# Attention and two gated layers on one core: new tables for the order, the engines and the buffer slots

## The chip, the cores and the metric

The kernel runs on one core of a Trainium2 chip. The metric is the device time of one execution in microseconds (us): the median of the runs is 578.70 us (three runs: 578.62, 578.70 and 579.78 us).

## The reference, cut to what matters

```python
def _attn_ref(q, k, v):                       # B, H, S, D = 2, 8, 768, 64
    block, window = 32, 16
    k_sum = k.reshape(B, H, nb, block, D).max(axis=3)
    v_sum = v.reshape(B, H, nb, block, D).mean(axis=3)
    scores_l = scale * q @ k^T   where |i - j| < window, else -1e9
    scores_s = scale * q @ k_sum^T + log(block)
    a = softmax(concat(scores_l, scores_s))
    return a @ concat(v, v_sum)

def _moe_ref(x, w_in, w_out):                 # 1536 tokens, 512 -> 2048 -> 512
    h = x @ w_in
    return (h * clip(h + 3, 0, 6) / 6) @ w_out

def _moe2_ref(x, w_in, w_out):
    h = x @ w_in
    return (h * cos(h)) @ w_out

reference = _moe2_ref(_moe_ref(tokens(_attn_ref(q, k, v))))
```

## The kernel before, in words

**Attention.** The host hands in the 768 positions of a head pair in 12 windows of 96 (64 and 16 on either side). `k_prep` (L516) makes for one pair of heads the block maxima of the keys: two DVE reductions into `ks` (L524); where the keys come as one row (`kp`), three copies lay the windows into `kw` (L534), and one copy spreads the 24 maxima behind each window (L537). `v_sums` and `fill` do the like for the values. `att` (L543) is one unit: the scores (L555) go into two PSUM banks `s`; `soft` (L598) adds the mask and takes a row minimum on DVE (L606, four a unit and pair), exponentiates on ACT (L614), adds a guard and inverts the sums on DVE (L623 and L624, the pair `invert`), and multiplies `e` by them, "the normalisation" (L629, POOL or DVE). TensorE transposes `e` into bank `t` (L569), ACT or DVE copies that to `pt` (L572), and L580 multiplies by the values into the single bank `o`; a copy to `xh` (L593) and a subtraction into `xl` (L595) split the result into two parts that TensorE can multiply at full rate.

**The two layers.** Every matmul of the layers is three (high by high, high by low, low by high; L745 to L747, L821, L973). Weights arrive packed, are unpacked by ACT (L675) and DVE (L679, L683), and split by `parts` (L689 copy, L690 subtraction). After a first product, `post` (L754) computes the gate on ACT and DVE and splits it (L798 copy, L800 subtraction). `g2` and `evac` accumulate the second product and add it to the running sums (L862); the last of these go to the output.

**What sets the order.** Nothing is scheduled on the chip or by the framework. The program makes 2,579 steps, each with the engines that may run it and a cost on each. `Plan.run` (L337) then takes the table `ORDER` entry by entry: entry `x` is step `x // 5`, issued on engine `x % 5` (0 TensorE, 1 ACT, 2 DVE, 3 POOL, 4 a DMA). Each engine runs what it was given in that order and waits there for its inputs. `SLOTS` says which of a class's buffers each step's buffer is. The costs in the `op(...)` calls were read by the search that wrote the tables; `run` looks only whether the engine is among those allowed:

```python
        for x in ORDER:
            o, e = self.ops[x // 5], ENGINES[x % 5]
            assert e in o.engs and not o.wait
            ...
            o.fn(e)
```

Loads go out on SyncE's queue, the identity and the first two queries on ACT's (L450, L462). TensorE starts on the layers' first products while attention still runs: the 65th TensorE entry of the table before starts at 57.55 us.

Of the kernel before, what the change touches and what calls it, by code (L numbers as in the profile page):

```python
# [29 lines left out]
HT = 2  # L30
# [34 lines left out]
def consts():  # L65
# [161 lines left out]
)  # L227
SLOTS = dict(
    kp="1001",
    ks="10011101",  # L230
    kw="20132013",
    z="201021021001200102101202",
# [128 lines left out]
def body(ctx: ExitStack, tc: tile.TileContext, q, k, kg, v, vf, w_in1, w_out1, w_in2, w_out2, ident_d, mask_d, avg_d, out):  # L361
# [181 lines left out]
    def att(b, h, ps, zs, prio):  # L543
# [46 lines left out]
        def got():  # L590
            return res.t[:, 0:n * HT * P].rearrange("p (x c) -> p x c", x=n)
# [482 lines left out]
```

## Time and profile before

| | |
|---|---|
| median of three runs | 578.70 us |
| the profiled execution's own time | 578.94 us |
| its span | 577.2 us |
| TensorE busy | 557.3 us (97%) |
| DVE busy | 462.5 us (80%) |
| ACT busy | 324.6 us (56%) |
| POOL busy | 263.6 us (46%) |

All rows are of this one execution; 1.7 us of its time lie outside the span. Busy time is the union of an engine's instructions. Instructions of one engine overlap a little at their ends: on DVE the next one of a pair is often shown to start some 80 ns before the one ahead of it has ended. A group's mean is its instructions' own duration, waits not counted. The granted clock of TensorE (PEclk) is a share of 2.4 GHz, so 0.5 is 1.2 GHz.

### The profile page before, as it was taken

What the parts mean: (1) busy time and instruction counts of PE and PEld (TensorE: products, weight loads), DVE (VectorE), ACT (ScalarE), POOL (GpSimd) and SP (SyncE); (2) the same over time, 40 slices, a digit from 0 to 9 for tenths busy, and PEclk for the clock granted to TensorE, in tenths of its full rate; (3) what the DMA queues carried; (4) which work ended last, traced back from release to release, by engine and by line L of the source; (5) the groups of instructions that cost most, each with busy time, mean ns of one, the idle gap of its engine ahead of it and who ended that gap; (6) DMA issues with size and microseconds to landing.
All of it is one profiled execution on the core that took longest, in us unless ns stands there. A gap on an engine that the chain in (4) does not pass through costs nothing.

```text
span 577.2 us, 9078 instructions
## 1 busy us (share of the span) xinstructions
PE 557.3 (97%) x3290; PEld 461.1 (80%) x3290; DVE 462.5 (80%) x912; ACT 324.6 (56%) x681; POOL 263.6 (46%) x250
## 2 busy tenths in 40 slices
PE   3878999999999999999999999999999999999997
PEld 2567988888888888888888878888888888888885
DVE  4999988898689548763999889994999779986762
ACT  4888887275534313443457667765656576554440
POOL 2657634463565106523357585533533355722410
PEclk9989999999999999999999999999999999999999
DMA  8879920111413203230230033230213102200023
GB/s 279 310 262 318 331 70 9 38 36 67 126 64 109 74 0 110 75 109 1 74 109 1 1 110 110 74 109 1 73 55 125 41 0 76 108 1 0 19 91 111
DMA packets 17901, 53.06 MB, mean 92 GB/s; under 512 B 2240, under 2 KB 5696, under 8 KB 17856
## 3 DMA queue, kind: packets, MB, share of 16 engines
q1 hardware_dynamic: 17424, 52.15, 26.4%
q8 instruction: 26, 0.43, 0.3%
q10 hardware_dynamic: 432, 0.33, 0.2%
q14 instruction: 19, 0.16, 0.1%
HBM read 49.32 MB, written 3.15 MB: 91 GB/s over the span
## 4 chain that ended last, share of the span: by engine, by line
PE 92%; DVE 4%; ACT 1%; DMA 1%; issue 0%; POOL 0%; SPq 0%; DVEq 0%
PE acc L821 25%; PE s L821 21%; PE t L973 10%; PE h L973 10%; PE h L745 4%; PE h L746 4%; PE h L747 4%; PE o L973 3%; PE t L569 2%; PE s L555 2%; PE o L580 1%; PE o L747 1%; PE t L747 1%; PE t L745 1%; PE o L745 1%; PE o L746 1%
## 5 line engine op out<-in xcount | busy, mean ns | idle before, releaser
L821 PE MATMUL acc<-g,wo 128*128 128x512 f32 (+1 forms) x384 | 90.5, 365 | 0.0
L415 POOL TENSOR_SCALAR g<-r 128x512 fp32r<-128x512 f32 (+1 forms) x48 | 35.2, 735 | 116.7 <-DVE r L796 62.3
L420 POOL TENSOR_TENSOR g<-r,g 128x512 fp32r<-128x512 f32 (+1 forms) x48 | 67.1, 1401 | 30.4 <-ACT g L413 28.6
L821 PE MATMUL s<-wo,g 128*128 128x512 f32 x288 | 76.0, 389 | 0.0
L821 PE MATMUL acc<-wo,g 128*128 128x512 f32 x288 | 75.7, 389 | 0.0
L821 PEld LDWEIGHTS acc<-g,wo 128*128 128x128 f32 x384 | 66.5, 188 | 11.4 <-issue 0.2
L821 PEld LDWEIGHTS acc<-wo,g 128*128 128x128 f32 x288 | 54.0, 188 | 11.5 <-DVE pc L862 0.4
L821 PEld LDWEIGHTS s<-wo,g 128*128 128x128 f32 x288 | 54.1, 188 | 11.2
L821 PE MATMUL s<-g,wo 128*128 128x512 f32 x240 | 62.7, 389 | 0.0
L675 ACT ACTIVATE cu<-raw 128x512 f32<-128x512 f32 x64 | 42.1, 667 | 24.0 <-DVE cf L683 14.0
L821 PEld LDWEIGHTS s<-g,wo 128*128 128x128 f32 x240 | 45.0, 188 | 9.4
L420 DVE TENSOR_TENSOR g<-r,g 128x512 fp32r<-128x512 f32 (+1 forms) x52 | 45.9, 887 | 6.9 <-POOL g L415 4.0
L683 DVE SCALAR_TENSOR_TENSOR cf<-cu,cf 128x512 uint32<-128x512 uint32 x64 | 50.0, 792 | 0.9 <-ACT cu L675 0.4
L420 POOL TENSOR_TENSOR wi<-cf,wi 128x512 fp32r<-128x512 f32 x28 | 41.2, 1477 | 16.9 <-ACT wi L413 14.9
L777 ACT ACTIVATE r<-r 128x512 f32<-128x512 f32 x48 | 30.1, 629 | 30.5 <-DVE r L784 30.2
L413 ACT ACTIVATE g<-r 128x512 fp32r<-128x512 f32 (+1 forms) x52 | 32.5, 625 | 21.9 <-DVE r L784 12.7
L973 PE MATMUL t<-sx,wi 128*128 128x512 f32 x168 | 44.4, 389 | 0.0
L745 PE MATMUL h<-xh,wi 128*128 128x512 f32 (+1 forms) x112 | 42.0, 375 | 0.3 <-DVE r L784 0.3
L614 ACT ACTIVATE e<-e,sm 128x120 f32<-128x120 f32 x96 | 36.8, 386 | 9.7 <-DVE sm L606 7.7
L973 PE MATMUL h<-xh,wi 128*128 128x512 f32 x112 | 41.1, 389 | 0.0
L746 PE MATMUL h<-xl,wi 128*128 128x512 f32 (+1 forms) x112 | 40.4, 360 | 0.0
L784 DVE SCALAR_TENSOR_TENSOR r<-n,r 128x512 f32<-128x512 int32 x48 | 39.5, 827 | 0.8
(149 smaller groups left out, 1245.5 us busy)
## 6 DMA issues: line engine op xcount, KB each, us to landing
raw<-in_w_in_dram SPq DMA_DIRECT2D x32, 512.0 KB, 4.1
raw<-in_w_out_dram SPq DMA_DIRECT2D x32, 512.0 KB, 3.6
vw<-in_v_dram SPq DMA_DIRECT2D x8, 768.0 KB, 6.7
kw<-in_kw_dram SPq DMA_DIRECT2D x4, 720.0 KB, 6.6
z<-in_q_dram SPq DMA_DIRECT2D x22, 128.0 KB, 4.3
out_dram<-part SPq DMA_DIRECT2D x8, 256.0 KB, 2.1
kp<-in_k_dram SPq DMA_DIRECT2D x4, 400.0 KB, 4.1
y<-in_vt_dram SPq DMA_DIRECT2D x4, 384.0 KB, 4.4
```

Source lines behind the costliest of these rows:

```text
L413: nc.scalar.activation(out=out, in_=in_, func=ACTF.Copy, scale=scale)
L415: eng[e].tensor_scalar(out=out, in0=in_, scalar1=scale, scalar2=0.0, op0=ALU.mult, op1=ALU.add)
L420: eng[e].tensor_tensor(out=out, in0=in0, in1=in1.bitcast(F32), op=ALU.subtract)
L614: lambda e, x=x: nc.scalar.activation(out=e_.t[:, x, :], in_=e_.t[:, x, :], func=ACTF.Exp, scale=-1.0, bias=sm.t[:, x:x + 1], accum_out=sm ...
L675: lambda e: nc.scalar.activation(out=u.t, in_=raw.t.bitcast(F32)[:, :, 1], func=ACTF.Prelu, scale=2.0 ** -112, alpha=2.0 ** 32),
L683: lambda e: nc.vector.scalar_tensor_tensor(out=f().bitcast(U32), in0=u.t.bitcast(U32), scalar=3, in1=f().bitcast(U32), op0=ALU.logical_shi ...
L745: nc.tensor.matmul(out=o, lhsT=wh, rhs=hi, start=(kk == 0), stop=False)
L746: nc.tensor.matmul(out=o, lhsT=wh, rhs=lo, start=False, stop=False)
L747: nc.tensor.matmul(out=o, lhsT=wl, rhs=hi, start=False, stop=(kk == KT - 1))
L784: op({"DVE": t(0.056, 0.542)}, lambda e: nc.vector.scalar_tensor_tensor(out=out(), in0=a(), scalar=s, in1=b(), op0=o0, op1=o1), pr, r=rd, ...
L821: nc.tensor.matmul(out=o, lhsT=l, rhs=r, start=(c == 0 and z == 0), stop=(c == GS - 1 and z == 2))
L973: nc.tensor.matmul(out=bank.t, lhsT=stat(u), rhs=get(v), start=(first and q == z == 0), stop=(q == 1 and z == 2), skip_group_check=True)
```

## The change

All 2,579 entries of `ORDER` and the strings of `SLOTS` are replaced, and seven costs that the search read are set anew. The steps themselves, their arithmetic and their shapes stay.

```diff
 ORDER = (
-    24, 174, 14, 59, 4, 64, 27, 36, 209, 32, 9, 324, 177, 186, 191, 182, 196, 42, 47, 18, 409, 202, 52, 214, 90, 644,
...
+    24, 59, 4, 174, 209, 64, 36, 47, 43, 27, 9, 32, 14, 409, 53, 18, 90, 182, 196, 188, 177, 193, 127, 324, 107, 202,
...
 SLOTS = dict(
-    kp="1001",
-    ks="10011101",
+    kp="0101",
+    ks="11010010",
...
-        op({"PE": 0.79}, mm, prio, mode=3, r=["avg", (vws[b, p], 0)], w=[bank], take=[bank, x, y])
+        op({"PE": 0.82}, mm, prio, mode=3, r=["avg", (vws[b, p], 0)], w=[bank], take=[bank, x, y])
...
-        op({"PE": 0.17 + 0.4 * n}, score, prio, mode=1,
+        op({"PE": 0.2 + 0.39 * n}, score, prio, mode=1,
...
-            op({"PE": 0.39}, trans, prio + 0.5 * AS * HT * x, r=["ident", *((e_, y) for y in range(N4))], w=[tp], take=[tp, pt])
+            op({"PE": 0.405}, trans, prio + 0.5 * AS * HT * x, r=["ident", *((e_, y) for y in range(N4))], w=[tp], take=[tp, pt])
...
-        op({"ACT": 0.1 + 0.207 * n, "DVE": 0.075 + 0.266 * n}, lambda e: copy(e, hi, got()), prio, r=[res],
+        op({"ACT": 0.26 + 0.12 * n, "DVE": 0.075 + 0.266 * n}, lambda e: copy(e, hi, got()), prio, r=[res],
...
-        op({"DVE": 0.16}, invert, prio, w=sums)
+        op({"DVE": 0.42}, invert, prio, w=sums)
         op(
-            {"POOL": 0.98, "DVE": 0.57},
+            {"POOL": 0.99, "DVE": 0.63},
...
-        op({"ACT": t(0.125, 0.45), "POOL": t(0.15, 0.47)}, lambda e: copy(e, hi(), r()), pr, r=[rb], w=[(gb, 0)],
+        op({"ACT": t(0.125, 0.45), "POOL": t(0.53, 0.1)}, lambda e: copy(e, hi(), r()), pr, r=[rb], w=[(gb, 0)],
```

Decoded by the rule above, the two tables say this.

**Entries by engine, whole table:** DVE 790, then 792; ACT 583, then 565; POOL 241, then 257; TensorE 841 and DMA 124 in both.

**Entries ahead of TensorE's 66th, where the two differ** (before, then after):

| steps | DVE | POOL | ACT |
|---|---|---|---|
| normalisation (L629) | 4, 1 | 8, 11 | |
| copy of `t` to `pt` (L572) | 3, 0 | | 9, 12 |
| weights' low part (L690) | 3, 1 | 4, 6 | |
| copy of `o` to `xh` (L593) | 1, 4 | | 8, 5 |
| windows into `kw` (L534) | 2, 3 | 4, 6 | 6, 3 |
| maxima into `kw` (L537) | 4, 3 | 2, 3 | |
| copy to `y` (L503) | 2, 3 | | 2, 1 |
| weights' high part (L689) | | 6, 4 | 2, 4 |
| gate's high and low part (L798, L800) | | 7, 5 | 1, 2 |
| mask and minimum (L606), exp (L614), gate (L777), unpack (L675) | 53, 52 | | 65, 61 |

TensorE's own first 65 entries are the same steps but for one, in nearly the same order.

**The first entries.** Before: the loads of the first two pairs' keys go out first, then identity, query, mask, values; DVE has the maxima of the first pair (two), of the second pair (two), two windows of the first pair (L534), the spread maxima (L537) of the second pair and then of the first; ACT has one window of the first pair and three of the second; POOL has the two further masks (L452). TensorE's first entry, the first pair's scores, needs the spread maxima and all windows of the first pair. After: the loads are the first pair's keys, its query, the mask, and only then the second pair's keys; DVE has one window of the first pair, its two maxima, and then the second pair's two maxima; POOL has one window of the first pair, its spread maxima, the masks, and then two windows of the second pair; ACT has one window of either pair.

**The normalisation and the fill near 31 us.** In both tables one pair's `invert` (step 151) and normalisation (step 152) are on DVE, and the fill of `vw` (step 141, L513) is on POOL just behind the latter. Before, step 152 comes straight after step 151; after, one unpacking (L679) stands between them.

**The end.** In both tables the last two entries are a whole addition of 512 columns into an output tile (L862) and its store, behind the last entry of TensorE's.

## Rows read from the trace of the kernel before

**Rows 1.** Stretches: us, busy us (x instructions) by engine, PEclk, DMA share, GB/s.

```profile
0.00:14.43 14.43, 5.34 (x72) 3.86 (x76) 7.00 (x33) 7.01 (x23) 3.90 (x15) 1.00 0.81 279
14.43:28.86 14.43, 12.09 (x234) 8.27 (x226) 13.03 (x62) 11.97 (x41) 9.77 (x10) 1.00 0.89 310
28.86:43.29 14.43, 11.32 (x165) 9.24 (x166) 13.62 (x53) 12.06 (x48) 8.07 (x8) 0.88 0.76 262
43.29:57.72 14.43, 12.97 (x181) 11.34 (x180) 14.29 (x54) 12.22 (x40) 11.11 (x14) 1.00 0.92 318
57.72:72.15 14.43, 14.43 (x190) 13.78 (x191) 14.15 (x53) 12.02 (x41) 8.81 (x11) 1.00 0.91 331
...
sum 577.20, PE 557.27 PEld 461.12 DVE 462.46 ACT 324.56 POOL 263.63; mean PE 13.93 PEld 11.53 DVE 11.56 ACT 8.11 POOL 6.59
```

**Rows 2.** What TensorE waited for, whole span: total us, times, longest.

```profile
PE s L555 <- DVE kw L417: 7.8, 1, 7.8
PE o L580 <- DVE xl L420: 2.0, 3, 1.0
PE t L569 <- ACT xh L413: 1.8, 1, 1.8
PE s L555 <- DVE sm L606: 1.8, 3, 1.0
```

**Rows 3.** Timeline of the start: start us, us, engine, line, operation.

```profile
4.36 1.01 DVE L524 TENSOR_REDUCE ks<-kp 128x12 f32<-128x384 f32 x2 [3.45 <-DMA kp<-in_k_dram]
...
5.65 1.01 DVE L524 TENSOR_REDUCE ks<-kp 128x12 f32<-128x384 f32 x2 [0.28 <-DMA kp<-in_k_dram]
...
6.58 0.69 DVE L417 COPY kw<-kp 128x384 f32<-128x384 f32 x2
...
7.19 0.51 DVE L417 COPY kw<-ks 128x288 f32<-128x288 f32 x2
...
7.81 1.08 PE L555 MATMUL s<-kw,z 64*64 64x120 f32 x16 [7.81 <-DVE kw L417]
```

**Rows 4.** Groups by line and shape up to 57.55 us: busy us, mean ns.

```profile
L629 POOL TENSOR_TENSOR e<-e,sm 128x480 f32<-128x480 f32 x8 | 8.5, 1060 | 11.7 <-DVE sm L624 6.2 <-DVE sm L606 4.7 <-ACT vs L413 0.7
...
L683 DVE SCALAR_TENSOR_TENSOR cf<-cu,cf 128x512 uint32<-128x512 uint32 x8 | 5.6, 698 | 0.0
...
L420 POOL TENSOR_TENSOR wi<-cf,wi 128x512 fp32r<-128x512 f32 x2 | 2.9, 1436 | 0.1
...
L415 POOL TENSOR_SCALAR kw<-kp 128x384 f32<-128x384 f32 x4 | 2.4, 610 | 0.0
...
L417 DVE COPY pt<-t 120x512 f32<-120x512 f32 x3 | 2.1, 684 | 0.1
...
L420 DVE TENSOR_TENSOR wi<-cf,wi 128x512 fp32r<-128x512 f32 x2 | 1.3, 659 | 0.0
L415 POOL TENSOR_SCALAR kw<-ks 128x288 f32<-128x288 f32 x2 | 1.1, 556 | 0.4 <-PE o L580 0.2
...
L417 DVE CAST xh<-o 128x256 fp32r<-128x256 f32 x1 | 0.4, 425 | 0.0
```

**Rows 5.** Line L629 up to 58 us: min/median/max ns, first and last start.

```profile
L629 DVE TENSOR_TENSOR e<-e,sm x4: 647/826/1799, 14.1 to 51.4; 128x480 f32<-128x480 f32 x4
```

**Rows 6.** Timeline about 31 to 35 us.

```profile
31.52 1.47 POOL L415 TENSOR_SCALAR vw<-vs 24x1536 f32<-24x1536 f32 x1
31.69 1.80 DVE L629 TENSOR_TENSOR e<-e,sm 128x480 f32<-128x480 f32 x1
...
33.64 1.08 PE L569 MATMUL t<-ident,e 128*120 128x128 f32 x4 [1.79 <-ACT xh L413]
```

**Rows 7.** Whole span by shape: a copy that more entries put on POOL.

```profile
L413 ACT ACTIVATE wi<-cf 128x512 fp32r<-128x512 f32 x43 | 26.8, 627 | 18.7 <-DVE cf L712 8.2 <-DVE cf L683 7.5 <-PE h L746 2.0
...
L415 POOL TENSOR_SCALAR wi<-cf 128x512 fp32r<-128x512 f32 x17 | 13.5, 794 | 23.6 <-DVE cf L683 15.1 <-DVE cf L712 8.4
```

**Rows 8.** The last DVE instruction of the span.

```profile
573.32 0.69 DVE L862 TENSOR_TENSOR pc<-pc,s 128x512 f32<-128x512 f32 x1 [0.67 <-PE s L821]
```

More of the change, by code (lines that the diff above doesn't have):

```diff
@@ L86 @@
 ORDER = (
[140 rows of a table removed]
[140 rows of a table added]
 )
 SLOTS = dict(
-    kp="1001",
-    ks="10011101",
-    kw="20132013",
-    z="201021021001200102101202",
-    vw="12030123",
-    h="1011100001010101101001100110100111011010100110101001101001100110",
+    kp="0101",
+    ks="11010010",
+    kw="10231023",
+    z="020122012001120102121002",
+    vw="31201320",
+    h="0101100001010101101010011000100110011010100110101001101001100110",
     vs="01011000",
     y="00000000",
-    s="011001011010100101100101101010011001101101010110100110101001101010011001100110011010010110",
@@ L238 @@
-    e="202012102101202102102102",
-    sm="323201201201302003030231",
+    s="101001011010010101010110011001101001101010010110011010100101101001100110010110011001101010",
+    e="102102102101021012012012",
+    sm="322302301323121031032102",
     t="00000000000000000000000000000000000000000000000",
-    pt="010101001010010101011001",
+    pt="101011010101100101101001",
     o="000000000000000000000000000000000000000",
-    raw="1021021210210212101201020121202102201201012012102112002120102021",
@@ L244 @@
-    cu="0110101010101011101101011010101101101101010101010110110001010100",
-    cf="0101010001210210120211020120101212012201102011020201220102120210",
-    wi="341025670413173250644172635027450634427053167451603271425630",
-    wo="21304231042310432104312403124031",
-    n=(
-        "1001011100111001201212101210101211101022101112001120120202212120121021012110210102210102210100120210"
-        "10120122102012"
-    ),
-    r="0010010111002002010122102020100122102101101202010120210210210120021020210121020101201201012020212021",
@@ L253 @@
-    g="1302102330126175042381657862031548672164573028641035728461386057823146807845136278504125687320172456",
-    acc="01011010101101101010010110010101011010011011010101010011",
-    pc="2404314130",
-    sx="520134",
+    raw="2012101210021200210210122121101220201210021012012001202120102021",
+    cu="1001001010111010011101101000010011101001100111001010101001010100",
+    cf="1010101110201201201200120121021001210012102011020201221001201021",
+    wi="043125437160302675146401237565170423216374050632751434026715",
@@ new lines @@
+    wo="24031204321404312043104231042310",
+    n=(
+        "0001000011102211212200200122111222110121021011202212110122021202010210100122012201212112102200012110"
+        "12121020120202"
+    ),
+    r="1010011101102211100202210220020111110202110102100210021002101021021002010212020112010121120121021012",
+    g="1230013202134712465807132156327845160841257301864260783156323510786453260412356817041283751024768345",
+    acc="10011010001110100011100101110111101010101010101010011010",
+    pc="3412041423",
@@ L257 @@
+    sx="423051",
 )
```

278 rows, old and new, of the table ORDER are left out of this document.

## The prediction, made before the changed kernel was run

> **What bounds the kernel now.** I read the stretches first. In the first four of 14.43 us TensorE is busy 5.34, 12.09, 11.32 and 12.97 us; in the fifth, and in every later one but the last, it is busy throughout [rows 1]. So of 57.72 us it works 41.72 and idles 16.0; of the remaining 519.5 us it idles 3.9, and the last DVE instruction starts at 573.32 us [rows 8], so that is the tail. The matmuls are the same in both kernels, so the change can win or lose in three places only: in the 16.0 us ahead of 57.72 us, in the 3.9 us behind 573.3 us, and by breaking the cover between them.
>
> The list of waits says who causes the 16.0 us: 7.8 is the time to the first score, the rest is in pieces of 1.8 us and less, released mostly by DVE [rows 2]. DVE is the loaded engine there: 7.00 + 13.03 + 13.62 + 14.29 = 47.9 us busy of the 53.4 that follow its first input at 4.36 us [rows 1, 3], or 90%, where POOL has 32.9 of the whole 57.7. One row wants a second look: the transposes at 33.64 us waited 1.79 us, by the list for an ACT copy, but the normalisation that they read ran on DVE from 31.69 for 1.80 us, beside a POOL fill from 31.52 for 1.47 us [rows 6]; alone, the same normalisation takes 0.65 us [rows 5]. The stretch from 28.86 us is also the one with a mean granted clock of 0.88 [rows 1]; with levels of 1 and 0.5 that is 0.24 × 14.43 = 3.5 us at 1.2 GHz, worth 1.7 us of full-speed work.
>
> **The change, part by part.** The seven costs are read by the search alone; at run time they are worth nothing. What runs otherwise is the tables.
>
> *The start.* Before, the first scores at 7.81 us stood behind eight DVE instructions: both pairs' maxima (4.36 to 5.37 and 5.65 to 6.66), two window copies to 7.27 and two spreads of the maxima to 7.70 [rows 3]. After, DVE does one window (half of 0.69) and the first pair's maxima (1.01), and the spread is POOL's, 0.56 [rows 3, 4]: 4.36 + 0.35 + 1.01 + 0.56 = 6.28, and with the 0.1 us between the last copy and the scores of before, 6.4 us. That is 1.4 us earlier. The nearest bounds: DVE's and POOL's first windows read the same tile together, and if one shuts the other out for POOL's 0.61 us [rows 4], the gain is 0.8; an earlier landing of the first keys, now ahead of the second pair's, would add, but no row prices it and I take 0. Behind the spread POOL has the masks, which DVE needs after the scores, 1.08 us long, so they are covered. The second pair's keys are issued two places later; they were used from 5.65 us, and DVE has work until 5.7, so a landing at up to 6.2 costs only the second scores, which in any case wait until DVE has emptied the score banks of the first. The next loads of keys wait for the first pair's buffer, free earlier by as much. I take 1.4.
>
> *The relief of DVE up to the 66th entry of TensorE (57.55 us).* By the table of entries DVE loses three copies to `pt` (3 × 0.684), three normalisations (3 × 0.647, the undisturbed one), two low parts (2 × 0.659) and one spread (0.26, half of 0.51): 5.6 us [rows 3, 4, 5]. It takes on three copies to `xh` (3 × 0.425), one window (0.35) and one copy to `y`, which has no row of its own and is smaller than that to `xh` (0.3): 1.9 us. Net 3.7; with four instructions fewer, the 0.08 us by which neighbours overlap is not saved four times: 3.4. As DVE is 90% loaded and releases most of TensorE's waits, I count the whole of it, with 0 and 3.4 as its bounds: 8.2 us of waiting lie there (16.0 − 7.8), so there is room. It is not the start's gain over again: DVE begins at 4.36 us either way, the start shortens its standing idle for the first scores, and the relief shortens its work.
>
> *What POOL takes on.* Three normalisations (1.06 each), two low parts (1.44), two windows (0.61), one spread (0.56), less two high parts (0.79 each) and two parts of the gate, for which I put the copy's 0.79 too [rows 4, 7]: 3.18 + 2.88 + 1.22 + 0.56 − 3.16 = 4.7 us more, on 32.9 of 57.7 us. POOL's own load does not bind. But rows 6 show a DVE instruction held for as long as a POOL instruction ran. DVE spends 5.6 us on the unpacking of L683, 4 × 0.826 on normalisations, 3 × 0.66 on low parts and 1.2 on copies from SBUF to SBUF [rows 3 to 5], 12 of 53.4 us on instructions that could meet such a hold; allowing for as much again that I cannot see, a third. A third of 4.7 is 1.6 us given back; bounds 0 and 4.7.
>
> The Trainium skill, "SBUF — State Buffer", section on the two separate sides, has a rule that speaks against this part: DVE and GpSimd share one pair of ports, and whichever of a two-input DVE instruction and a GpSimd instruction starts second stands still for the whole of the first. Rows 6 agree (0.65 became 1.80 beside 1.47). By that rule alone work moved to POOL still holds the pair, and longer than on DVE; its full price is the slower rival below.
>
> *The same collision near 31 us.* Step 152 stays on DVE and the fill on POOL, so I leave its 1.15 us and the clock's 1.7 us in the sum. *ACT* loses five instructions net and gains none on a path that TensorE waited for: nothing. *TensorE's order* is nearly the same: nothing. *Loads:* same bytes; the DMA engines run at shares of 0.76 to 0.92 there [rows 1]; nothing in the sum, a bound in a rival.
>
> *From 57.72 to 573.3 us.* Sixteen entries more on POOL and 18 fewer on ACT in the whole table, mostly copies of high parts, 0.79 instead of 0.63 us [rows 7]. They hide under TensorE, which was never idle there, with POOL busy 46% of the span. If the cover broke wherever eleven of them moved, it would be 11 × 0.17 = 1.8 us. I take nothing. *The tail* ends with the same full-width addition and its store: nothing.
>
> **Sum.** −1.4 − 3.4 + 1.6 = −3.2 us, on the profiled execution's 578.94 us: 575.7. The median is 0.24 us below that execution, so the forecast is 575.5 us.
>
> **Rivals.** *The collision near 31 us goes too.* The search had the pair of L623 and L624 at 0.16 us and now has 0.42, so it may now keep the fill apart. For: step 152 is still listed ahead of the fill. Against: an unpacking now stands between steps 151 and 152, which makes 152 later. It would save 1.15 us and the clock's 1.7 more: 572.7 us. Chance 0.18.
>
> *Only the start counts.* The middle waits stay as they are, since loads and ACT (12 of 14.43 us in each of three stretches [rows 1]) hold the pace as soon as DVE does not: 578.7 − 1.4 = 577.3 us. Chance 0.12.
>
> *Nothing comes of it.* The start's gain is lost where the second pair's later keys hold up the next scores, and DVE's relief is idle time: 578.7 us. Chance 0.11.
>
> *POOL stands in DVE's way.* Place: the 53 us from 4.36, where POOL's 4.7 us more all fall against DVE instructions, as in rows 6; price 4.7, and one further drop of the clock like that of the third stretch, 1.7. −1.4 − 3.4 + 4.7 + 1.7 = +1.6: 578.7 + 1.6 = 580.3 us. It decides from 4.8 us of DVE time held, less where a drop of the clock comes with it. For: rows 6 and the rule above. Against: DVE would have to want the pair whenever POOL has it, and by rows 4 it does so a third of the time at most. Chance 0.14.
>
> **How the numbers follow.** The forecast has 0.45. What a measurement of this kernel can tell from no change is about 0.2%, 1.16 us, so faster means below 577.5 us. The forecast and the first rival lie there, and most of the second (0.10 of 0.12): 0.73. No change: the third rival, the rest of the second and a little of the last, 0.14. Slower: 0.13. Range: up to 578.8, which takes in all but the slower rival; down to 572.6, which takes in the first rival; left out 0.13 above and some 0.05 below. Cases of both signs do not share the chance evenly, so the forecast needs no range of its own.
>
> **What would show it.** Right: the first scores at 6.3 to 6.5 us, or 7.0 if the two first windows collide; TensorE idle 12 to 13.5 us ahead of the first full stretch instead of 16.0; DVE's busy time ahead of TensorE's 66th entry near 44.5 us instead of 47.9; that entry at 54 to 54.6 us; no wait of TensorE from there to the end; the tail unchanged at 3.9 us. Wrong: normalisations and unpackings on DVE of 1.3 us and more in several places beside POOL instructions; a new stretch with a clock under 0.9; a TensorE wait behind 60 us; or waits for transposes released by POOL of more than the few tenths that they are now.

## The result and the profile after

The changed kernel takes 582.19 us (median of 15 runs, 580.28 to 584.59) where the kernel before takes 578.76 (578.51 to 579.78): a ratio of 1.0054, 95% interval 1.0045 to 1.0063. It is slower by 0.54%, 3.4 us; the forecast was 575.5 and the range ended at 578.8. The profiled execution is one of 582.19 us with a span of 580.3, 3.2 us above the span before.

The stretches of the changed kernel, in the columns of [rows 1], the first four and then three from the middle:

```profile
0.00:14.43 14.43, 5.67 (x77) 3.87 (x78) 6.84 (x32) 6.33 (x21) 5.93 (x18) 1.00 0.82 274
14.43:28.86 14.43, 12.10 (x228) 8.38 (x224) 13.87 (x63) 11.78 (x41) 11.06 (x12) 1.00 0.83 300
28.86:43.29 14.43, 11.02 (x156) 9.08 (x156) 14.17 (x52) 11.13 (x43) 9.88 (x9) 0.78 0.85 289
43.29:57.72 14.43, 13.95 (x190) 12.66 (x189) 13.41 (x50) 12.68 (x39) 11.06 (x14) 0.98 0.84 311
...
317.46:331.89 14.43, 14.02 (x62) 11.33 (x61) 12.76 (x20) 10.63 (x19) 7.51 (x7) 1.00 0.00 0
331.89:346.32 14.43, 13.91 (x60) 10.83 (x59) 14.05 (x23) 9.16 (x16) 6.17 (x6) 1.00 0.33 111
346.32:360.75 14.43, 14.15 (x62) 11.35 (x62) 13.56 (x18) 9.26 (x16) 12.14 (x10) 1.00 0.21 73
```

The same three stretches of the kernel before:

```profile
317.46:331.89 14.43, 14.43 (x65) 11.88 (x64) 12.84 (x20) 10.06 (x18) 8.01 (x8) 1.00 0.00 1
331.89:346.32 14.43, 14.43 (x64) 11.42 (x63) 12.75 (x20) 9.68 (x17) 11.73 (x10) 1.00 0.32 110
346.32:360.75 14.43, 14.43 (x66) 11.94 (x65) 14.33 (x23) 11.07 (x20) 8.41 (x7) 1.00 0.33 110
```

Two things are to be seen. The first 57.72 us hold 42.7 us of TensorE's work instead of the 41.7 of [rows 1], but 3.4 us more of it at 1.2 GHz (mean granted clock 0.78 and 0.98 in the third and fourth stretch, where it was 0.88 and 1.00). And in these three stretches of the middle, where TensorE was busy 14.43 us of every 14.43 with 64 to 66 matmuls, it now gets through only 60 to 62.

To place a loss I use TensorE's **lag**: the start of a step of TensorE less the summed listed costs of all TensorE steps ahead of it, in the same listed costs for every kernel. Where it stands still, TensorE is kept waiting by nobody and runs at full clock. Worked out from the traces, in us (the experiments' columns are used further down):

```
at about, us    before  after    x1     x2     x3     x4     x5     x6     x7     x8     x9    x10    x11    x12
  6             7.81   5.92   5.99   7.78   5.90   5.86   6.02   6.11   5.96   7.54   5.99   6.05   5.82   5.98
 12            10.83  10.35   9.58  10.80   9.03   9.92   9.00   9.52   9.78  10.57   9.12   9.42  10.35  10.69
127            27.36  27.28  26.93  27.12  26.59  26.15  26.10  26.58  28.01  26.61  25.73  26.51  25.43  28.27
287            27.35  27.29  26.93  27.13  26.61  26.14  26.10  26.60  28.02  26.60  25.72  26.52  25.45  28.29
339            27.87  29.45  27.49  29.35  28.79  26.14  26.62  30.96  31.92  26.60  26.25  26.52  27.65  30.52
430            27.87  30.67  27.49  30.54  30.02  26.14  26.64  31.79  33.06  26.60  26.25  26.52  28.88  31.33
```

The head starts 1.9 us earlier and is level with before at 127 us (27.28 against 27.36). What the head comes to differs between executions of one program: x1, x6, x7, x10 and x12 have the changed kernel's entries up to 127 us, and their lag there lies between 26.51 and 28.27. So two columns that differ by a few tenths at 127 us show nothing by that alone; from 287 us on, the rise is the same to about 0.1 us wherever the entries of the middle are the same (3.38 in the changed kernel, 3.41 in x2 and x3). From 287 to about 391 us the lag rises by 3.4 us, where before it rose by 0.5. The rest of the 3.2 us of span, 0.36, is in the tail: the last DVE addition now starts 4.2 us before the end, 3.9 before [rows 8].

TensorE's waits over the whole span (us, times, longest), beside [rows 2]:

```profile
PE s L555 <- POOL kw L415: 5.9, 1, 5.9
PE o L580 <- DVE xl L420: 2.9, 2, 1.5
PE s L555 <- issue: 2.8, 1, 2.8
```

The first scores wait 5.9 us, now for POOL, instead of 7.8. A second wait of 2.8 us is new. The middle does not show in this list, since TensorE loses its time there in small pieces, and first at its weight loads. What these waited for from 288 to 392 us:

```profile
PEld acc L821 <- DVE pc L862: 0.9, 1, 0.9
PEld t L973 <- DVE o L981: 0.8, 2, 0.5
PEld t L973 <- DVE sx L420: 0.8, 1, 0.8
```

With three more groups of 0.7, 0.4 and 0.4 us that is 4.0 us, all of it for DVE (one more wait, of 0.2, is for ACT, none for POOL); before there were two of 0.35 and 0.32 us. The chain of work that ended last says the same, before and then now:

```profile
PE 92%; DVE 4%; ACT 1%; DMA 1%; issue 0%; POOL 0%; SPq 0%; DVEq 0%
```

```profile
PE 74%; DVE 18%; issue 3%; ACT 2%; POOL 1%; DMA 1%; SPq 0%; DVEq 0%; ACTq 0%; POOLq 0%
```

What DVE is doing there, on the timeline from 314 us (start, duration, engine, line, operation):

```profile
314.07 1.74 POOL L874 TENSOR_TENSOR part<-part,part 128x512 f32<-128x512 f32 x1
314.59 1.78 DVE L420 TENSOR_TENSOR g<-r,g 128x512 fp32r<-128x512 f32 x1
...
315.77 1.75 POOL L420 TENSOR_TENSOR sx<-part,sx 128x512 fp32r<-128x512 f32 x1
...
316.89 1.19 DVE L420 TENSOR_TENSOR sx<-part,sx 128x512 fp32r<-128x512 f32 x1
...
318.13 0.73 PE L973 MATMUL t<-sx,wi 128*128 128x512 f32 x2 [0.41 <-DVE sx L420]
```

DVE's subtraction of the gate takes 1.78 us beside a POOL addition of 1.74 and one of POOL's subtractions, and its next one 1.19. In x10 (below), where POOL's subtractions are memsets, two such subtractions together take 1.29, 0.65 each, while a POOL memset runs:

```profile
314.35 1.70 POOL L425 MEMSET wi<- 128x512 f32 x3
...
315.26 1.29 DVE L427 TENSOR_TENSOR g<-r,g 128x512 fp32r<-128x512 f32 x2
```

This is the collision of [rows 6], far behind the head where I had looked for it. TensorE waits for the result of the second: its weight load 0.83 us, its matmul 0.41.

The start (to compare with [rows 3]):

```profile
5.92 1.08 PE L555 MATMUL s<-kw,z 64*64 64x120 f32 x16 [5.92 <-POOL kw L415]
7.67 1.01 DVE L524 TENSOR_REDUCE ks<-kp 128x12 f32<-128x384 f32 x2 [2.32 <-DMA kp<-in_k_dram]
8.60 0.27 DVE L606 CUSTOM_DVE_ANT_0 e<-s,mask 128x120 f32<-128x120 f32 x1
9.81 1.08 PE L555 MATMUL s<-kw,z 64*64 64x120 f32 x16 [2.82 <-issue]
```

The first scores start at 5.92 us. But the second pair's keys, now issued two places later, are used from 7.67 (5.65 before); their maxima stand on DVE ahead of the first masks, which so start at 8.60 though their scores ended at 7.0; and the second scores start at 9.81 (9.85 before). In this execution the 1.9 us are gone within four microseconds. In the eight traces with these first entries (the changed kernel, x1, x4, x6, x7, x10, x11 and x12) the second scores start anywhere from 8.89 to 10.15 us, so a part of the lead is sometimes left. And about 34 us:

```profile
31.58 0.65 DVE L629 TENSOR_TENSOR e<-e,sm 128x480 f32<-128x480 f32 x1
...
33.66 1.28 POOL L420 TENSOR_TENSOR wi<-cf,wi 128x512 fp32r<-128x512 f32 x1
33.73 1.75 DVE L683 SCALAR_TENSOR_TENSOR cf<-cu,cf 128x512 uint32<-128x512 uint32 x1
...
35.96 0.69 PE L580 MATMUL o<-pt,vw 120*64 120x64 f32 x16 [1.47 <-DVE xl L420]
37.69 1.27 POOL L420 TENSOR_TENSOR wo<-cf,wo 128x512 fp32r<-128x512 f32 x1 [1.36 <-ACT wo L413]
37.92 1.58 DVE L683 SCALAR_TENSOR_TENSOR cf<-cu,cf 128x512 uint32<-128x512 uint32 x1
```

The normalisation of [rows 6] now starts ahead of the fill and runs undisturbed in 0.65 us, as the first rival had it. In its place two unpackings (0.70 in [rows 4]) take 1.75 and 1.58 us beside the weights' low parts that the new table gave to POOL, and TensorE waits 1.47 us behind the first. From 37.0 us TensorE then runs at 1.2 GHz for 6.8 us, where before it did so for 3.4 us from 33.5.

### The profile page after: what moved, and what is told of

The parts are those of the page before. It is cut to its first block, busy times and chain, and to the rows that moved or that the text cites. A ratio compares the mean times of both kernels' runs of the same rounds, so it can differ in the third digit from the quotient of the medians.

```text
span 580.3 us, 9081 instructions
## 1 busy us (share of the span) xinstructions
PE 559.8 (96%) x3290; PEld 461.7 (80%) x3290; DVE 471.8 (81%) x914; ACT 311.7 (54%) x663; POOL 271.0 (47%) x266
## 4 chain that ended last, share of the span: by engine, by line
PE 74%; DVE 18%; issue 3%; ACT 2%; POOL 1%; DMA 1%; SPq 0%; DVEq 0%; ACTq 0%; POOLq 0%
PE acc L821 20%; PE s L821 16%; PE t L973 8%; PE h L973 7%; DVE r L784 3%; PE h L745 3%; PE h L747 3%; PE h L746 3%; PE o L973 3%; PE s L555 2%; DVE cf L683 2%; PE o L580 2%; PE t L569 2%; DVE g L420 2%; DVE cf L679 1%
## 5 line engine op out<-in xcount | busy, mean ns | idle before, releaser
L821 PE MATMUL acc<-g,wo 128*128 128x512 f32 (+1 forms) x384 | 92.0, 365 | 0.0
L420 POOL TENSOR_TENSOR g<-r,g 128x512 fp32r<-128x512 f32 (+1 forms) x46 | 59.9, 1304 | 51.3 <-ACT g L413 49.6
L675 ACT ACTIVATE cu<-raw 128x512 f32<-128x512 f32 x64 | 42.5, 668 | 38.6 <-DVE cf L683 18.8
L683 DVE SCALAR_TENSOR_TENSOR cf<-cu,cf 128x512 uint32<-128x512 uint32 x64 | 55.2, 865 | 1.2 <-ACT cu L675 0.4
L420 DVE TENSOR_TENSOR g<-r,g 128x512 fp32r<-128x512 f32 (+1 forms) x54 | 49.9, 929 | 5.8 <-POOL g L415 3.7
L777 ACT ACTIVATE r<-r 128x512 f32<-128x512 f32 x48 | 30.2, 630 | 43.3 <-DVE r L784 43.3
L420 POOL TENSOR_TENSOR wi<-cf,wi 128x512 fp32r<-128x512 f32 x25 | 36.9, 1478 | 20.8 <-ACT wi L413 20.2
L745 PE MATMUL h<-xh,wi 128*128 128x512 f32 (+1 forms) x112 | 42.4, 379 | 0.2 <-DVE r L784 0.2
L614 ACT ACTIVATE e<-e,sm 128x120 f32<-128x120 f32 x96 | 36.8, 386 | 10.4 <-DVE sm L606 8.5
L747 PE MATMUL h<-xh,wi 128*128 128x512 f32 (+1 forms) x112 | 40.6, 362 | 0.0
```

Of the source, the lines that this page charges most:

```text
L420: eng[e].tensor_tensor(out=out, in0=in0, in1=in1.bitcast(F32), op=ALU.subtract)
L614: lambda e, x=x: nc.scalar.activation(out=e_.t[:, x, :], in_=e_.t[:, x, :], func=ACTF.Exp, scale=-1.0, bias=sm.t[:, x:x + 1], accum_out=sm ...
L675: lambda e: nc.scalar.activation(out=u.t, in_=raw.t.bitcast(F32)[:, :, 1], func=ACTF.Prelu, scale=2.0 ** -112, alpha=2.0 ** 32),
L683: lambda e: nc.vector.scalar_tensor_tensor(out=f().bitcast(U32), in0=u.t.bitcast(U32), scalar=3, in1=f().bitcast(U32), op0=ALU.logical_shi ...
L745: nc.tensor.matmul(out=o, lhsT=wh, rhs=hi, start=(kk == 0), stop=False)
L747: nc.tensor.matmul(out=o, lhsT=wl, rhs=hi, start=False, stop=(kk == KT - 1))
```

## Experiments

### The table cut in two

x1 takes the first 850 entries (to about 145 us) of the new table and then what is left in the old order; x2 the other way round. Slots follow the order.

```diff
 ORDER = (
     ... 4047, 4021, 4180,
-    4472, 3968, 4350, 3942, 4521, ...
+    3942, 3968, 3946, 4350, 4521, ...
```

> The first 850 entries are the new table's, the other 1729 follow the old table (buffers renamed to fit). My theory: the time is lost between 288 and 391 us, by the new table's own work there, and the new head is worth about nothing; then TensorE has no lag over the kernel before at 400 us (within 0.5 us) and the median is 578 to 579.5 us, swinging by the length of the slow-clock stretch of the head. Rival: the loss is laid by the head (what it leaves late is paid at 290 us), then the median stays at 581 us or above.

> The first 850 entries are the old table's, the others follow the new one. My theory: TensorE's lag over the kernel before grows by 2 to 3 us between 288 and 391 us and by nothing elsewhere; median 581 to 582 us with little swing, since the old head has its own short slow-clock stretch. Rival (the head lays the loss): 578.5 to 579.5 us.

x1: 579.32 us, ratio 1.0011 [0.9997, 1.0025]; x2: 581.97, 1.0061 [1.0048, 1.0074]. x1's lag rises by 0.56 us in the middle, x2's by 3.4. The loss belongs to the new middle, and needs nothing of the new head. By the medians the new head is worth +0.4 us (579.32 against 578.90 for the kernel before, measured beside it; the interval takes in no change) and the rest of the new table +3.1 (581.97 against 578.90).

### POOL's subtractions without their reads

In x4, in all 99 of the changed kernel's POOL subtractions, three memsets of the output tile stand in for the subtraction (three, so that POOL is occupied about as long); left out are the low parts that POOL computes. x8 is the same edit on the kernel before; x10 does it only for the 30 that run between 270 and 400 us, x11 only for the first 11, all before 60 us.

```diff
     def sub(e, out, in0, in1):
+        if e == "POOL":
+            for _ in range(3):
+                nc.gpsimd.memset(out.bitcast(F32), 0.0)
+            return
```

> The new tables; every subtraction on POOL (the low parts) is replaced by three memsets of the same tile, so POOL writes for about as long but reads nothing (left out: the low parts that POOL makes, set to zero). Theory of the shared port: DVE instructions of 1.3 us and more beside POOL's subtractions go, DVE's busy time falls by 20 us or more of 471.8, the lag of 2.8 us between 288 and 391 us goes and so do the waits at 33 to 36 us; 577 to 579 us. Rival (the order of DVE's own work loses the time, whatever POOL does): DVE's long instructions may shrink but the lag of 2 to 3 us stays; 581 to 582 us.

> The kernel before with POOL's subtractions replaced by memsets, the control of the like run of the new tables (left out: the low parts that POOL makes, set to zero). Contention theory: the old tables suffer as many holds, but with slack behind them; DVE's busy time falls by 20 us or more here too (from 462.5), the time by only the 0.5 us lost at 332 us and up to 1.5 us in the first 60: 577 to 578.5 us. If the gain is as large as that of the new tables (5.7 us), holds are a tax on both and say nothing of their difference: 573.5 us.

> The new tables, with POOL's subtractions replaced by three memsets of the same tile only for the 30 of them that run between 270 and 400 us (leaves out those low parts). Theory (POOL's reads hold DVE there, and TensorE waits for it): TensorE's lag no longer rises between 288 and 391 us (2.8 us before), the head stays as in the changed kernel, and the run gives 582.2 - 2.9 = 579.3. Rival (x4's gain came from a head that gets ahead and stays ahead, or from the load on DVE over the whole run): above 581.

> The new tables, with the memsets only in place of POOL's first 11 subtractions, all before 60 us (leaves out those low parts). Theory: the head gains what x4 gained there (lag at 100 us about 1.2 less than in the changed kernel) and the loss of 2.8 us between 288 and 391 us stays as it is: 581. Rival (a lead at 60 us carries through the middle as slack): 579 or less.

x4: 576.47 us, ratio 0.9961 [0.9949, 0.9974], 5.7 us below the change and under the 577 to 579 expected. x8: 578.16, 0.9989 [0.9980, 0.9998]. x10: 578.5, 0.9990 [0.9980, 1.0000]. x11: 579.98, 1.0025 [1.0016, 1.0035]. The page's busy times, of the changed kernel and of x4:

```profile
PE 559.8 (96%) x3290; PEld 461.7 (80%) x3290; DVE 471.8 (81%) x914; ACT 311.7 (54%) x663; POOL 271.0 (47%) x266
```

```profile
PE 556.8 (97%) x3290; PEld 461.0 (80%) x3290; DVE 440.1 (76%) x914; ACT 311.3 (54%) x663; POOL 278.9 (48%) x464
```

POOL is busier, and DVE, with the same 914 instructions, does them in 31.7 us less. With only the middle so treated (x10), TensorE is never idle there, no weight load waits, and its lag stands at 26.52 from 127 us to the end:

```profile
317.46:331.89 14.43, 14.43 (x65) 11.97 (x64) 12.94 (x22) 11.79 (x20) 6.68 (x12) 1.00 0.00 1
331.89:346.32 14.43, 14.43 (x65) 11.94 (x65) 14.07 (x24) 9.06 (x17) 5.41 (x10) 1.00 0.31 110
346.32:360.75 14.43, 14.43 (x66) 11.94 (x65) 11.56 (x20) 9.07 (x15) 10.12 (x17) 1.00 0.21 74
```

The groups by shape from 288.6 to 389.6 us say on which DVE instructions the time lay (busy us, mean ns), first the changed kernel, then x10, whose lines are numbered 7 higher:

```profile
L420 DVE TENSOR_TENSOR g<-r,g 128x512 fp32r<-128x512 f32 x12 | 14.2, 1203 | 0.3 <-ACT g L413 0.2
L683 DVE SCALAR_TENSOR_TENSOR cf<-cu,cf 128x512 uint32<-128x512 uint32 x14 | 12.3, 881 | 0.2
...
L874 DVE TENSOR_TENSOR part<-part,part 128x512 f32<-128x512 f32 x7 | 6.8, 967 | 0.0
```

```profile
L690 DVE SCALAR_TENSOR_TENSOR cf<-cu,cf 128x512 uint32<-128x512 uint32 x14 | 9.9, 705 | 1.3 <-ACT cu L682 1.2
...
L427 DVE TENSOR_TENSOR g<-r,g 128x512 fp32r<-128x512 f32 x13 | 8.6, 682 | 0.2 <-ACT g L413 0.2
...
L881 DVE TENSOR_TENSOR part<-part,part 128x512 f32<-128x512 f32 x7 | 5.3, 758 | 0.0
```

The gate's subtraction falls from 1203 to 682 ns, the sum of two tiles from 967 to 758, the unpacking (L683) from 881 to 705; over these seven stretches DVE is busy 85.7 us instead of 96.4. A memset also drops the wait for the subtraction's inputs, so in principle a shorter chain through POOL could have helped. Against that stand the weight loads' waits above, none of which is for POOL, and DVE's idle time of tenths in these rows.

x10's median is 3.7 us below the change's, where 2.9 was expected. Of the 4.1 us between the two profiled executions (578.05 against 582.19), 3.4 lie in the middle and 0.8 in a shorter head (26.51), though the two programs are the same up to 270 us. x11 tells the other half: its median is 2.2 us below the change's, its head 1.85 us shorter, with no stretch at 1.2 GHz there, and yet the middle costs it 3.4 us as before (25.45 to 28.88). So a lead from the head is no slack for the middle; that rival falls, though 579.98 us lies between the 581 and the 579 that were expected. The two parts add up to the whole: 3.7 and 2.2 are 5.9, where x4 gains 5.7.

x8 shows that the old table suffers from the same holds and hardly pays for them. There the memsets take DVE from 462.5 to 436.9 us of busy time, and from 94.8 to 85.3 in the seven stretches, 9.5 us, where the new table has 10.7 (96.4 to 85.7). Yet the old middle had only 0.5 us to lose by them, and the new one loses 3.4. So how long DVE is held in all does not tell the two tables apart.

### Engines or order

x6 puts back two things of the middle that the new table took from DVE's partners: four evacuations of L851 from DVE to ACT and two additions of L874 from DVE to POOL. x12 does only the evacuations. x7 gives some 60 entries of the middle their old engines, in the new order.

```diff
-    ... 7067 ... 7097 ... 8397 ... 8347 ... 8642 ... 9017 ...
+    ... 7068 ... 7098 ... 8396 ... 8346 ... 8641 ... 9016 ...
```

> The new tables with six steps behind 270 us put back on their old engine at the same place in the order: four copies out of the accumulator (L851) from DVE to ACT, two additions (L874) from DVE to POOL. Load theory (DVE is full between 290 and 400 us, and every instruction put on it there costs its own length): DVE loses 4 x 0.6 + 2 x 0.87 = 4.1 us of work, the lag of 2.9 to 3.4 us falls to 1 to 1.5 us, median near 580.5. Contention theory (the holds by POOL alone cost the time): DVE's instructions stay as long as they are, two more on POOL, lag of 3 us or more, median 582.

> The new order throughout, but every step that ran between 270 and 400 us is on the engine that the old table gave it (58 steps moved back). If the choice of engines loses the time: lag over the kernel before 0.7 us or less at 400 us, median 579.5 to 580. If the order on the engines loses it: lag of 2 us and more stays, 581.5 to 583.

> The new tables with only the four evacuations of L851 after 270 us put back on ScalarE, as in x6, but the two additions of L874 left on VectorE. If the two additions on POOL made x6 slower than the change (three tensor-tensor operations in a row on POOL beside DVE's), this gives 581 to 582.2; if the evacuations on ScalarE did, 584 as x6.

x6: 584.3 us, ratio 1.0102 [1.0085, 1.0118]; x7: 584.65, 1.0097 [1.0083, 1.0111]; x12: 581.83, 1.0046 [1.0033, 1.0060]. DVE has less to do (four and six instructions fewer in x12 and x6; 91.5 us busy in the seven stretches of x7, against 96.4), and none gains clearly: x12 is level with the change, x6 is slower by 2.1 us and x7 by 2.5. In the middle their lags rise by 3.0 (x12), 5.2 (x6) and 5.0 us (x7), where the change has 3.4. "DVE has too much to do" falls, and so does the choice of engines by itself, as x7 loses more with the old engines in the new order. x6 and x7 lie above both of the times that were expected for them. x6's timeline, where TensorE waits:

```profile
314.26 2.99 POOL L874 TENSOR_TENSOR part<-part,part 128x512 f32<-128x512 f32 x2
...
317.22 1.73 POOL L420 TENSOR_TENSOR sx<-part,sx 128x512 fp32r<-128x512 f32 x1
...
317.73 3.44 DVE L420 TENSOR_TENSOR g<-r,g 128x512 fp32r<-128x512 f32 x2
...
318.91 1.71 POOL L420 TENSOR_TENSOR xl<-part,xh 128x512 fp32r<-128x512 f32 x1
...
321.22 0.73 PE L821 MATMUL acc<-g,wo 128*128 128x512 f32 x2 [1.69 <-DVE g L420]
```

With the two additions on POOL, its subtractions move back beside DVE's two subtractions of the gate, which take 3.44 us together where one alone takes 0.68, and TensorE waits 1.69 us behind them. The same two additions sat on POOL before, in another order, and cost nothing. At this place, then, what counts is which instruction of POOL stands beside which of DVE, and how long TensorE can do without that one; for the rest of the middle that is argued from it and from x7. Why the old order has this slack, step by step, I did not settle.

### The head

x3 issues the second pair's keys right behind the first's. x5 does that in x1, so a new head with the early keys before the old rest. x9 is x5 with the two low parts of L690 that held the unpackings put back on DVE, each behind the unpacking it held.

```diff
-    24, 59, 4, 174, 209, ...
+    24, 174, 59, 4, 209, ...
...
-    ... 921, 2507, 2488, 771, 637, ...
+    ... 921, 2507, 771, 637, 2487, ...
...
-    ... 2577, 2664, 2518, ...
+    ... 2577, 2517, 2664, ...
```

> The new tables with one load moved: the second pair's keys go out right behind the first pair's, ahead of the first query and the mask. My theory: they land by 6 us instead of 7.6, DVE does not stand idle from 5.4 to 7.7, the first mask steps start near 7.2 instead of 8.6 and TensorE's second scores near 8.4 instead of 9.8 us. The 1.3 us carry to the end only if the waits near 33 to 40 us and the slow clock behind them do not eat them: 580.5 to 582 us against 582.2. Rival (the landing is set by the bytes in flight, not by the place in the queue): second scores again at 9.8 us, no change.

> New head with the second pair's keys loaded right behind the first pair's, and the old table from entry 850 on. If both findings add: TensorE's lag at 100 us is 0.5 to 0.8 us under that of the kernel before, nothing is lost at 288 to 391 us beyond the old table's own 0.5 us, and the median is 577.5 to 578.5 us, faster than either kernel. Rival (the head's waits and slow clock eat any earlier start): 578.9 us and above.

> The kernel of x5 (second keys first, new head of 850 entries, old rest) with the two subtractions of L690 that the new tables gave to POOL at 32.4 and 36.4 us put back on DVE, right behind the L683 that each of them held. Theory (those two subtractions cost the head its lead): both L683 fall from 1.75 and 1.58 us to under 0.9, DVE pays 2 x 0.66 for the subtractions, TensorE's two late steps at 34.7 and 39.1 us (1.73 and 2.28 late) shrink by about 1 us each, and the run gives 576.5 to 577.5. Rival (POOL's next instruction moves up and holds DVE instead, or DVE is full either way): 578.2 as x5.

x3: 581.4 us, ratio 1.0044 [1.0032, 1.0057]; x5: 578.17, 0.9987 [0.9975, 0.9999]; x9: 577.34, 0.9982 [0.9970, 0.9994]. With the early keys the second scores start at 8.55 to 8.68 us in all three, where the late keys gave 8.89 to 10.15. How much of that is left at 127 us the single traces cannot say (26.59 in x3, 26.10 in x5, 25.73 in x9, against 26.51 to 28.27 without the move). By the medians x5 is 1.2 us below x1, and their intervals only just meet; x3 is 0.8 below the change, within the spread. x9's unpackings:

```profile
32.51 0.66 DVE L683 SCALAR_TENSOR_TENSOR cf<-cu,cf 128x512 uint32<-128x512 uint32 x1
...
33.42 1.14 DVE L420 TENSOR_TENSOR wi<-cf,wi 128x512 fp32r<-128x512 f32 x1
...
36.67 0.69 DVE L683 SCALAR_TENSOR_TENSOR cf<-cu,cf 128x512 uint32<-128x512 uint32 x1
```

Both fall to under 0.7 us, one of the returned subtractions takes 1.14 beside a POOL normalisation, and the lag at 127 us is 0.37 below x5's. The two steps did not gain the us apiece that I expected: TensorE's step at 33.65 us is 0.64 late instead of 1.73, but the scores near 39 us are still 2.9 late. x9 beats both kernels: its interval lies below 1, and its median 4.9 us below the change's. Its 0.8 us below x5 are not clear of the spread, as the two intervals overlap.

## Why the prediction was wrong

The forecast was 575.5 us and the measurement 582.2. x1 and x2 divide the 6.7 us between them: the head, forecast at −3.2 us, came out at +0.4, and the rest, forecast at nothing, at +3.1. So two steps failed.

**The first: "From 57.72 to 573.3 us … I take nothing".** It held the cover to be safe because TensorE was never idle there, and bounded the loss by what a moved copy costs POOL itself, 0.17 us apiece, 1.8 us in all. But the engine that the cover hangs on is DVE, and DVE had little to spare: before, it was busy 12.8 to 14.3 us of each 14.43 in the seven stretches from 288.6 us. In place of nothing the runs showed 2.9 us of waiting over the old table (3.4 against 0.5): POOL's subtractions hold DVE's instructions, and in the new order TensorE waits for the held ones. x2 shows that this comes with the new middle, x10 that it goes when POOL's subtractions become memsets, and x12, x6 and x7 that it goes neither with DVE's load nor with the engines alone. The sixteen entries more on POOL, which the step priced, are not the cause: in the seven stretches POOL is busy 57.8 us, against 60.1 before, and has 24 subtractions instead of 26. What differs is which instructions meet, and what waits behind them; why the old order stayed clear of it is open.

**The second: the head's sum, −1.4 − 3.4 + 1.6.** *The start*, "I take 1.4": it was 1.9 at the first scores, and 0 at the second in the profiled execution (from 1.0 gained to 0.3 lost in the eight traces). I had allowed the second keys to land at up to 6.2 us at no cost; here they were used from 7.67, and their maxima stood ahead of the first masks on DVE's queue. That queue position was in the table, and I did not read it.

*The relief of DVE, −3.4, and POOL's holds, +1.6.* TensorE's 66th entry starts at 56.8 us, where I expected 54 to 54.6 (57.55 before). Up to it DVE is busy 47.4 us, against 47.8 before, and TensorE idle 15.0 against 16.0. The copies, normalisations and low parts did leave DVE, but what stayed there in the same number took longer. Up to the 66th entry, before and then after (L683 before: [rows 4]):

```profile
L623 DVE TENSOR_SCALAR sm<-sm 128x4 f32<-128x4 f32 x12 | 4.4, 369 | 1.4 <-ACT e L614 1.4
...
L679 DVE TENSOR_SCALAR cf<-raw 128x512 uint32<-128x512 uint32 x8 | 3.4, 420 | 0.0
```

```profile
L683 DVE SCALAR_TENSOR_TENSOR cf<-cu,cf 128x512 uint32<-128x512 uint32 x8 | 7.4, 929 | 0.1
...
L623 DVE TENSOR_SCALAR sm<-sm 128x4 f32<-128x4 f32 x12 | 5.8, 483 | 1.2 <-ACT e L614 1.2
...
L679 DVE TENSOR_SCALAR cf<-raw 128x512 uint32<-128x512 uint32 x8 | 4.9, 618 | 0.0
```

That is 1.8 + 1.4 + 1.5 = 4.7 us: the mis-sized term is "+1.6, a third", and its upper bound of 4.7 the better figure. The third did not follow from its own working either, as 12 of 53.4 us and as much again is 0.45. In x11 the unpackings of L683 are back at 5.4 us, so POOL's subtractions held those; L679 and L623 stay long there (5.3 and 5.8 us). In the trace they stand beside POOL's other work (one L679 takes 1.01 us from 22.34, beside a normalisation from 22.09), but no run took that work away, so their holder is argued and not shown.

**The rival that came true in kind.** "POOL stands in DVE's way" gave 580.3 us and the right sign. Its place was only half right: I confined it to the 53 us of the head, because only there did TensorE wait in the profile of before. The holds were in the old middle too (x8), hidden, as nothing waited for them. The rule of the Trainium skill, "SBUF — State Buffer", section on the two separate sides, which I weighed for the head alone, is borne out in the middle: 0.68 became 1.78 beside 1.74.

**What held.** The first scores' release by POOL; the collision of [rows 6], which the first rival said would go, and it did, without the gain, as two others took its place. The tail was to be unchanged and is 0.36 us longer; it comes with the later part of the new table (3.85 us in x1, 4.14 in x2), and its cause is open.

## What to carry to other kernels

Where a fixed order is replaced as a whole, cost it wherever the engine that feeds the bound one is nearly full, not only where the bound engine waits now: a cover of nothing shows no wait until it breaks. The price of work on GpSimd beside a loaded VectorE is the hold on the neighbour, and here it depended on the pair that met and not on the load; replacing the reads by memsets of the same length shows that price in one run. And where a searched table loses in one stretch and not in another, cut it: the new head with two repairs on the old rest (x9) had the lowest median of the kernels that compute the whole result.

## What the runs showed of the hardware

A memset on POOL does not hold a DVE subtraction as a POOL subtraction does: in x10 the DVE subtractions of the gate took 682 ns on average among POOL memsets that last 1.70 us for three, and 1203 in the changed kernel among POOL subtractions of 1.5 us. It is not so for every DVE instruction: the unpacking's L679, which reads one tile, took 0.72 us at 28.30 us in x11, beside three memsets from 28.23, and 0.42 at 28.29 in the changed kernel, where it started ahead of POOL's instruction.

A wait costs more on TensorE than its length when the granted clock falls after it. The changed kernel ran at 1.2 GHz for 6.8 us from 37.0 us, just behind the 1.47 us wait that ended at 35.96. Which of the head's waits the clock falls behind differs between executions: x1, x6 and x10, with the same entries there, ran at 1.2 GHz for 3.4 us from about 41 us. x4 and x11 have the same memsets in the head; x4 ran at 1.2 GHz for 3.4 us from 24.2, x11 not at all there, and x11's lag at 127 us is 0.7 us shorter (25.43 against 26.15). The 15 runs of the changed kernel spread with it: the two slowest, 583.24 and 584.59 us, have a mean granted clock of 0.991, the three with 0.999 and more take 580.28 to 581.13.
